# Score steps of the first three tiles in single PSUM banks, four in flight, in place of two bank pairs

## The chip, the cores and the metric

The kernel runs on one core of a Trainium2 chip. The metric is device time in microseconds (us), the median of several runs. All times of a trace count from the start of its span. The engines are named as in the profile: PE (TensorE matmuls), PEld (its weight loads), DVE (VectorE), ACT (ScalarE), POOL (GpSimd), SP (SyncE, which here issues the DMAs).

## What is computed

Block-causal attention, then a mixture of four experts, then one dense layer with a softmax gate and a layer norm:

```python
scores = scale * q @ k.T, masked by blocks of 64 (i >= j)     # 4 batches, 8 heads, 576 positions, width 64
attn = exp(scores - max) / (sum + 1e-9);  x = attn @ v        # x: 2304 x 512
out = sum over 4 experts e of p[:, e] * (relu(x @ w1[e]) @ w2[e])      # 512 -> 1024 -> 512
h = out @ w_in;  solu = h * softmax(h);  y = layernorm(solu) * g @ w_out
```

## The kernel before

The 2304 rows are 18 tiles of 128. `TILES[t] = (b, i)`: tiles 0 and 1 take the first 64 positions of two batches each (i = 0), tile 2 is (0, 1), tile 3 is (0, 2), tile 4 is (0, 3), tile 5 is (0, 4), and so on. A tile is computed in attention steps: tiles 0 and 1 have two steps of four heads (steps 0 to 3), tile 2 has four steps of two heads (4 to 7), tile 3 has steps 8 to 11, tile 4 has 12 to 15, and tile 5 has eight steps of one head (16 to 23).

A step has three parts. `step_a` multiplies q with k on PE into the PSUM tile `sps` (a high and a low part of q, L902 and L903 in tiles 0 and 1, L920 and L923 later, and a masking product); then DVE takes the maximum (L932 or L935, written into free words of the same PSUM tile) and turns it into the exponent's bias `nm` (L939). `step_b` lets ACT do the exponential head by head (L979); while `t < DIRECT`, with `DIRECT = 3`, the result goes back in place into PSUM. ACT copies it to half precision in `hl` (L992), DVE subtracts for the rest (L993), and SP transposes `hl` by DMA into `pT`. `step_c` multiplies `pT` with v on PE (`pv`, L1021). After the last step of a tile, `finish` normalises it on DVE (L1057 to L1063), splits it (`xh`, L1074 on ACT, L1075 on DVE), and SP transposes it into `xT`.

The scores go through a pool of two PSUM tiles of two banks each; a step gives its tile back when its last subtraction L993 has run. `hl` has two buffers (`hlp=2`), q has four (`qp=4`).

As soon as tiles are ready, the experts' matmuls fill PE between the steps: `emit_h` (`hps`, L375: 96 matmuls for one tile, 128 columns each) and `emit_o` (`ops`, L397: 24 matmuls of 512 columns for one tile). Their weights are loaded into `stage`, squared on ACT for a scale (L132), summed (L217), multiplied by ones on PE (`tp`, L219), turned into `ws` on DVE (L221, L136, L140, L143), and split in four chunks: the high part `wt` on POOL (L231) for the first expert and on ACT (L235) for later ones, the low part on DVE (L238). POOL also converts q and k (`qhi`, `qlo`, `ks`, L798 and L800) and v (L881; its low part on DVE is L882).

The program's order up to tile 2 is a hand-written string of tokens; then a planner mixes attention steps and expert units by their costs. The framework's scheduler then sets each engine's instruction order from a simulated timeline and the priorities of that program order. Each engine runs its own list strictly in that order.

Of the kernel before, what the change touches and what calls it, by code (L numbers as in the profile page):

```python
# [7 lines left out]
F32 = mybir.dt.float32  # L8
# [9 lines left out]
PSUM = bass.MemoryType.PSUM  # L18
# [14 lines left out]
DIRECT = 3  # L33
# [30 lines left out]
def tile_kernel(  # L64
# [19 lines left out]
    class InOrder:  # L84


        def __init__(self, eng):
            self.eng, self.last = eng, None
# [655 lines left out]
    class Attention:  # L744


        def __init__(self, bufs):
            self.es = es = ExitStack()
            self.nraw = {k: bufs[k] for k in ("qr", "kr")}
            for n, k in bufs.items():  # L750
                setattr(self, n, es.enter_context(tc.tile_pool(name=n, bufs=k)))
            self.pss = es.enter_context(tc.tile_pool(name="pss", bufs=2, space=PSUM))
            self.psv = es.enter_context(tc.tile_pool(name="psv", bufs=4 - NPH, space=PSUM))
            self.kS, self.qS, self.vS, self.vSc, self.raws = {}, {}, {}, {}, {}
            self.sPS, self.hl_, self.nm_, self.pT_, self.sums, self.xps = {}, {}, {}, {}, {}, {}
            self.steps = []
            for t in range(NTILE):
                i = TILES[t][1]
                if i == 0:
                    self.steps += [(t, c, tuple(range(4 * c, 4 * c + 4)), True) for c in range(2)]  # L760
                elif i < 4:
                    self.steps += [(t, p, (2 * p, 2 * p + 1), True) for p in range(4)]
                else:
                    for p in range(4):
                        self.steps += [(t, p, (2 * p,), False), (t, p, (2 * p + 1,), True)]
            self.first = {}
            for n, st in enumerate(self.steps):
                self.first.setdefault(st[0], n)
            self.NS = len(self.steps)
            self.fin = []  # L770
            self.n = self.na = self.nb = self.nc = self.nhl = 0
            self.todo = []
            self.plan()

            self.todo.sort(key=lambda x: x[0])
            self.loads = {k: [l for _, (x, l), _ in self.todo if x == k] for k in self.nraw}
            self.nl = {k: 0 for k in self.nraw}
            self.done = {k: 0 for k in self.nraw}
# [107 lines left out]
        def step_a(self, n):  # L886
            t, p, heads, _ = self.steps[n]
            b, i = TILES[t]
            ps = self.pss.tile([128, 2, 512], F32, tag="s", name="sps")
            self.sPS[n] = ps  # L890
            nm = sp.tile([128, 4], F32, tag="nm", name="nm")
            self.nm_[n] = nm
# [35 lines left out]

            def rest():
                if i == 0:  # L930
                    mx = ps[:, 1, 0:4]
                    vec.tensor_reduce(out=mx, in_=v4, axis=AX.X, op=ALU.max, negate=True)  # L932
                elif i < 4:
                    mx = ps[:, :, 511]
                    vec.tensor_reduce(out=mx, in_=ps[:, :, 0:L], axis=AX.X, op=ALU.max, negate=True)  # L935
                else:
                    mx = nm[:, 0:1]
                    vec.tensor_reduce(out=mx, in_=ps[:, :, 0:288], axis=AX.XY, op=ALU.max, negate=True)
                vec.tensor_scalar(  # L939
                    out=nm[:, 0:nh], in0=mx, scalar1=SCALE, scalar2=PBITS * LN2, op0=ALU.mult, op1=ALU.add  # L940
                )
# [317 lines left out]
    def norm():  # L1259
# [11 lines left out]
        w=p0[:5], x=p1[:5], W=p0[5:] + q0, X=p1[5:] + q1, P=[norm],  # L1271
# [108 lines left out]
    while at1.more:  # L1380
        t, u, cost = moe[-1] if moe else (-1, None, 0)
        ok = t is None or t in ready and len(bg) <= n1
        if not ok or tdv <= tpe + 2.0:
            flush()
            at1.step()
            a, c = at1.cost()
# [233 lines left out]
```

## Time and profile before

| | |
|---|---|
| median of 3 runs | 1090.99 us (1089.95 to 1091.23) |
| the profiled execution | 1090.29 us, its span 1088.5 us |
| PE busy | 1041.5 us, 96% of the span |
| DVE, ACT, POOL busy | 776.3, 511.1, 208.1 us |

The profiled execution is 0.70 us below the median of the runs, and 1.79 us of it lie outside the span. A row of the timeline gives the start, the duration, the engine and line, what is written and read, how many instructions are merged into the row, and in brackets how long the engine stood idle before it and what ended that.

### The profile page before, as it was taken

The numbers are of one execution on the slowest core, as the hardware profiler recorded it, in microseconds if no ns is written. First come the engines' busy times: TensorE is split into PE (matmuls) and PEld (weight loads), VectorE is DVE, ScalarE is ACT, GpSimd is POOL, SyncE is SP. The second block draws the span as 40 slices with busy tenths as digits, with TensorE's granted clock in tenths as the row PEclk, the third lists the DMA queues.
The fourth block names the chain that finished last, engine by engine and source line by source line (L and its number), as shares of the span: only waits on it lengthen the run. The fifth ranks groups of instructions, "written<-read, shape, count | busy, mean of one in ns | idle before, by whom it ended". The sixth has DMA issues, their size and how long they took to land.

```text
span 1088.5 us, 20680 instructions
## 1 busy us (share of the span) xinstructions
PE 1041.5 (96%) x8088; PEld 657.0 (60%) x8088; DVE 776.3 (71%) x1758; ACT 511.1 (47%) x1108; POOL 208.1 (19%) x280
## 2 busy tenths in 40 slices
PE   4679899999999999999899999999999999999998
PEld 4556666656655655655476777776766674444444
DVE  6879677748767765545786557665879558999883
ACT  5757578546755454532353334231446353323322
POOL 4967733534237311000000000000000000000000
PEclk9989999999999999999999999999999999999999
DMA  9978997566677865235331211330346312435233
GB/s 295 277 175 167 241 201 189 143 173 172 158 178 174 186 112 129 56 90 157 122 97 51 77 47 55 117 136 30 98 145 167 77 24 36 88 88 106 60 87 87
DMA packets 225745, 137.96 MB, mean 127 GB/s; under 512 B 184560, under 2 KB 193008, under 8 KB 225648
## 3 DMA queue, kind: packets, MB, share of 16 engines
q1 hardware_dynamic: 225648, 136.65, 50.3%
q8 instruction: 63, 1.03, 0.4%
q14 instruction: 34, 0.28, 0.1%
HBM read 79.47 MB, written 12.06 MB: 84 GB/s over the span
## 4 chain that ended last, share of the span: by engine, by line
PE 84%; DMA 6%; DVE 4%; POOL 3%; ACT 1%; issue 1%; SPq 0%; DVEq 0%; ACTq 0%; POOLq 0%
PE ops L397 31%; PE hps L629 14%; PE hps L375 14%; PE o L1536 9%; PE h L1470 9%; PE pv L1021 3%; DMA pT<-hl 3%; PE sps L920 2%; PE sps L923 2%; DMA xT<-xh 1%; POOL ks L800 1%; DMA raw<-in_w_dram 1%; DMA x2T<-xh 1%; DMA near<-in_kT_dram 1%; DMA vraw<-in_vC_dram 1%
## 5 line engine op out<-in xcount | busy, mean ns | idle before, releaser
L397 PE MATMUL ops<-wt,hch 128*128 128x512 f16 x1728 | 393.1, 379 | 2.4 <-DVE wt L238 1.4
L397 PEld LDWEIGHTS <-hch 128*128 128x128 f16 x1728 | 166.1, 98 | 187.4 <-issue 6.7
L375 PE MATMUL hps<-xT,wt 128*128 128x384 f16 (+1 forms) x1536 | 216.1, 290 | 6.3 <-DVE hch L386 3.9
L375 PEld LDWEIGHTS <-wt 128*128 128x128 f16 x1536 | 126.5, 100 | 64.4 <-issue 6.1
L979 ACT ACTIVATE p<-sps,nm 128x320 f32<-128x320 f32 (+3 forms) x120 | 70.1, 587 | 85.1 <-DVE nm L939 75.4
L993 DVE TENSOR_TENSOR hl<-p,hl 128x320 f16<-128x320 f32 (+3 forms) x120 | 75.6, 650 | 37.3 <-ACT hl L992 37.2
L629 PEld LDWEIGHTS <-S 128*128 128x128 f16 x1152 | 96.0, 98 | 3.0 <-issue 0.9
L1536 PE MATMUL o<-wt,lt 128*128 128x512 f16 (+1 forms) x456 | 95.6, 368 | 0.0
L1470 PE MATMUL h<-wt,x2T 128*128 128x512 f16 x432 | 95.5, 379 | 0.0
L238 DVE SCALAR_TENSOR_TENSOR wt<-stage,ws,wt 128x1024 f16<-128x1024 f32 (+1 forms) x64 | 82.9, 1304 | 7.4 <-ACT wt L235 4.3
L422 DVE SCALAR_TENSOR_TENSOR acc<-ops,coef,acc 128x512 f32<-128x512 f32 x54 | 40.4, 748 | 66.4 <-PE ops L397 66.3
L920 PE MATMUL sps<-ks,qhi 128*128 128x288 f32 (+3 forms) x160 | 69.1, 433 | 10.7 <-DVE hl L993 7.5
L629 PE MATMUL hps<-T,S 128*128 128x192 f16 x864 | 76.3, 246 | 0.0
L629 PEld LDWEIGHTS <-wt 128*128 128x128 f16 x864 | 72.8, 98 | 5.8
L642 ACT ACTIVATE stu<-hps 128x384 f32<-128x384 f32 x72 | 34.6, 482 | 86.5 <-PE hps L629 86.3
L1536 PEld LDWEIGHTS <-lt 128*128 128x128 f16 x456 | 44.6, 98 | 48.9
L1470 PEld LDWEIGHTS <-x2T 128*128 128x128 f16 x432 | 42.3, 98 | 51.0
L386 DVE SCALAR_TENSOR_TENSOR hch<-hps,hch 128x384 f16<-128x384 f32 (+1 forms) x98 | 52.8, 540 | 21.9 <-ACT hch L385 21.8
L647 ACT ACTIVATE hch<-stc 128x384 f16<-128x384 f32 x72 | 37.4, 521 | 63.5 <-DVE stc L655 63.2
L385 ACT ACTIVATE hch<-hps 128x384 f16<-128x384 f32 (+1 forms) x98 | 46.9, 481 | 39.5 <-PE hps L375 39.4
L1021 PE MATMUL pv<-v,pT 128*128 128x64 f16 x1392 | 56.6, 196 | 8.9 <-DMA pT<-hl 8.8
L1021 PEld LDWEIGHTS <-pT 128*128 128x128 f16 x1392 | 51.6, 100 | 20.5 <-DMA pT<-hl 10.8
(163 smaller groups left out, 1534.6 us busy)
## 6 DMA issues: line engine op xcount, KB each, us to landing
stage<-in_w_dram SPq DMA_DIRECT2D x50, 512.0 KB, 5.9
raw<-in_qT_dram SPq DMA_DIRECT2D x34, 256.0 KB, 3.1
vraw<-in_vC_dram SPq DMA_DIRECT2D x30, 256.0 KB, 3.2
raw<-in_kT_dram SPq DMA_DIRECT2D x24, 288.0 KB, 3.5
raw<-in_w_dram SPq DMA_DIRECT2D x24, 256.0 KB, 4.1
raw<-in_w_in_dram SPq DMA_DIRECT2D x8, 512.0 KB, 4.7
raw<-in_w_out_dram SPq DMA_DIRECT2D x8, 512.0 KB, 4.2
stage<-wf SPq DMA_DIRECT2D x8, 512.0 KB, 6.6
```

What stands on the lines that cost most here:

```text
L238: stage["last"] = vec.scalar_tensor_tensor(out=lo, in0=r, scalar=stage[key, "s"], in1=hi, op0=ALU.mult, op1=ALU.subtract)
L375: pe.matmul(ps[:, j * n:j * n + n], w[:, a, kk, f * 128:(f + 1) * 128], x[:, b * KD + kk, c0:c0 + n], start=(m == 0), stop=(m == 3 * KD - 1),)
L385: marks["A"] = nc.scalar.activation(out=h[:, 0, :n], in_=ps[:, :n], func=AF.Relu)
L386: marks["D"] = nc.vector.scalar_tensor_tensor(out=h[:, 1, :n], in0=ps[:, :n], scalar=0.0, in1=h[:, 0, :n], op0=ALU.max, op1=ALU.subtract)
L397: pe.matmul(ps, hch[f][:, a, o0:o0 + 128], w[:, b, f, :], start=(m == 0), stop=(m == 3 * KF - 1))
L629: i = pe.matmul(ps[x][:, jj * HT:jj * HT + HT], lhs(a, kk, jj), rhs(b, kk), start=start, stop=(m == 5), skip_group_check=not first or jj > 0,)
L920: pe.matmul(o, q, rhs, start=True, stop=False)
L979: act.activation(out=src if direct else dst, in_=src, func=AF.Exp, bias=nm[:, j + x:j + x + 1], scale=SCALE, accum_out=sums[:, h:h + 1],)
L993: anc["D"] = vec.tensor_tensor(out=lo, in0=pf, in1=hi, op=ALU.subtract)
L1021: pe.matmul(o, tt[:, a * nch + c, :], v[:, bb, hs], start=(m == 0), stop=(m == total - 1))
L1470: pe.matmul(ps[:, half], x[:, a * KD + kk, c:c + 128], w[:, b, kk, half * 512:half * 512 + 512], start=(m == 0), stop=(m == 3 * KD - 1),)
L1536: pe.matmul(ps, tt[:, x * KF + f], w[:, y, f, c], start=(m == 0), stop=(m == 3 * KF - 1))
```

## The change

In tiles 0 to 2 a step now takes one PSUM bank from a new pool of four. In tiles 0 and 1 it needed only one bank anyway (four heads of 128 columns), and its maximum goes to `nm` in SBUF. In tile 2 the two heads of 192 columns lie side by side in one bank, and the two maxima in that bank's last two words. When the first step of tile 3 is built, the pool of single banks is closed, and the former pool of two bank pairs is opened over the same four banks.

```diff
-            self.pss = es.enter_context(tc.tile_pool(name="pss", bufs=2, space=PSUM))
             self.psv = es.enter_context(tc.tile_pool(name="psv", bufs=4 - NPH, space=PSUM))
+            self.one = ExitStack()
+            self.ps1 = self.one.enter_context(tc.tile_pool(name="ps1", bufs=4, space=PSUM))
+            self.pss = None
...
-            ps = self.pss.tile([128, 2, 512], F32, tag="s", name="sps")
+            spare = None
+            if t < DIRECT:
+                bank = self.ps1.tile([128, 512], F32, tag="s", name="sps")
+                w = 1 if i == 0 else 2
+                ps = bank[:, 0:512 if i == 0 else 128 + 256 * i].rearrange("p (a c) -> p a c", a=w)
+                if i:
+                    spare = bank[:, 510:512]
+            else:
+                if self.pss is None:
+                    self.one.close()
+                    self.pss = self.es.enter_context(tc.tile_pool(name="pss", bufs=2, space=PSUM))
+                ps = self.pss.tile([128, 2, 512], F32, tag="s", name="sps")
...
                 if i == 0:
-                    mx = ps[:, 1, 0:4]
+                    mx = nm
...
-                    mx = ps[:, :, 511]
+                    mx = ps[:, :, 511] if spare is None else spare
```

The scheduler answers with another order of instructions on all engines for the first part of the program (lines below `step_a` are 13 higher in the change, and those above it 2 higher). Three places matter here.

On DVE, where the first expert's scale `ws_207` is made: `wt1_311` is the sum of the squares, `v_277` the low part of tile 1's values, `hl_337` the remainder of step 2. Before:

```order
L217 TENSOR_REDUCE wt1_311<-wt4_206 128x1
L882 SCALAR_TENSOR_TENSOR v_277<-qv_137,vs_257,v_277 128x512
L221 COPY wt2_315<-tp_313 128x1
L136 TENSOR_SCALAR iw_93<-wt2_315 128x1
L140 TENSOR_SCALAR iw_93<-iw_93 128x1
L143 RECIPROCAL ws_207<-iw_93 128x1
L573 RECIPROCAL ss_7190<-iw_93 128x1
L573 RECIPROCAL ss_7391<-iw_93 128x1
L993 TENSOR_TENSOR hl_337<-sps_320,hl_337 128x512
```

The same place in the change (`sps_549` belongs to step 5):

```order
L948 TENSOR_REDUCE sps_549<-sps_549 128x2
L952 TENSOR_SCALAR nm_494<-sps_493 128x2
L143 RECIPROCAL vs_257<-vinv_258 128x1
L217 TENSOR_REDUCE wt1_311<-wt4_206 128x1
L952 TENSOR_SCALAR nm_550<-sps_549 128x2
L221 COPY wt2_315<-tp_313 128x1
L884 SCALAR_TENSOR_TENSOR v_277<-qv_137,vs_257,v_277 128x512
L136 TENSOR_SCALAR iw_93<-wt2_315 128x1
L1006 TENSOR_TENSOR hl_337<-sps_320,hl_337 128x512
L140 TENSOR_SCALAR iw_93<-iw_93 128x1
L143 RECIPROCAL ws_207<-iw_93 128x1
```

The maxima of steps 4 and 5 now come before the scale, and the two long instructions `v_277` and `hl_337` stand inside its chain.

On DVE again, at the first step of tile 3 (step 8: `sps_777`, `nm_778` before, `sps_781`, `nm_782` in the change); `wt_560` are chunks of w2 of the first expert. Before:

```order
L935 TENSOR_REDUCE sps_777<-sps_777 128x2
L386 SCALAR_TENSOR_TENSOR hch_780<-hps_779,hch_780 128x256
L238 SCALAR_TENSOR_TENSOR wt_560<-stage_268,ws_270,wt_560 128x1024
L939 TENSOR_SCALAR nm_778<-sps_777 128x2
L935 TENSOR_REDUCE sps_876<-sps_876 128x2
```

In the change:

```order
L1006 TENSOR_TENSOR hl_703<-sps_651,hl_703 128x192
L238 SCALAR_TENSOR_TENSOR wt_560<-stage_268,ws_270,wt_560 128x1024
L948 TENSOR_REDUCE sps_781<-sps_781 128x2
L238 SCALAR_TENSOR_TENSOR wt_560<-stage_268,ws_270,wt_560 128x1024
L952 TENSOR_SCALAR nm_782<-sps_781 128x2
L948 TENSOR_REDUCE sps_880<-sps_880 128x2
```

Before, the bias of step 8 stood behind the third of the four chunks; now it stands behind the fourth, and behind the last remainder of tile 2 (`hl_703`, step 7).

On PE, at the last step of tile 3 (step 11: `sps_982` before, `sps_986` in the change); `xT_477` holds tiles 0 to 2, `hps_1034` is tile 1, `pv_956` and `pv_960` are tile 3's products with v. Before:

```order
L375 LDWEIGHTS wt_415
L375 MATMUL hps_1034<-xT_477,wt_415 128x128
L920 MATMUL sps_982<-ks_443,qhi_763 128x320
L1021 LDWEIGHTS pT_825
L1021 MATMUL pv_956<-v_648,pT_825 128x64
```

In the change (`ops_1286` is tile 1's output product):

```order
L1034 LDWEIGHTS pT_829
L1034 MATMUL pv_960<-v_459,pT_829 128x64
L933 MATMUL sps_986<-ks_440,qhi_763 128x320
L936 MATMUL sps_986<-ks_440,qlo_764 128x320
L938 LDWEIGHTS mr_88
L938 MATMUL sps_986<-mc_89,mr_88 128x64
L933 MATMUL sps_986<-ks_443,qhi_763 128x320
L936 MATMUL sps_986<-ks_443,qlo_764 128x320
L938 LDWEIGHTS mr_88
L938 MATMUL sps_986<-mc_89,mr_88 128x64
L397 LDWEIGHTS hch_1126
L397 MATMUL ops_1286<-wt_560,hch_1126 128x512
```

Before, step 11 stood in the middle of tile 1's `hps` and was itself split by the product `pv` of step 8. In the change it stands behind all 96 `hps` of tile 1, behind the first 9 of its 24 `ops`, and behind that `pv`.

## Rows read from the trace of the kernel before

**Rows 1.** The page, part 1: busy time, share of the span, instructions of each engine.

```profile
PE 1041.5 (96%) x8088; PEld 657.0 (60%) x8088; DVE 776.3 (71%) x1758; ACT 511.1 (47%) x1108; POOL 208.1 (19%) x280
```

**Rows 2.** Stretches: bounds, length; PE, PEld, DVE, ACT, POOL busy; clock, DMA share, GB/s.

```profile
0.00:45.00 45.00, 20.96 (x130) 19.10 (x131) 33.25 (x90) 30.62 (x89) 28.65 (x38) 1.00 1.01 293
...
52.50:72.50 20.00, 13.16 (x124) 8.54 (x122) 16.29 (x29) 11.54 (x33) 18.61 (x18) 0.96 0.62 131
72.50:77.50 5.00, 5.00 (x48) 4.44 (x48) 2.73 (x5) 3.31 (x10) 2.01 (x4) 0.50 1.17 299
77.50:90.00 12.50, 12.50 (x142) 8.46 (x142) 9.23 (x19) 9.11 (x26) 2.53 (x4) 0.99 0.98 207
90.00:120.00 30.00, 27.72 (x400) 22.72 (x399) 28.96 (x62) 22.56 (x47) 25.95 (x33) 1.00 0.82 205
120.00:152.00 32.00, 26.36 (x356) 20.20 (x355) 21.47 (x54) 15.64 (x54) 21.02 (x33) 1.00 1.11 221
152.00:1088.50 936.50, 928.34 (x6805) 566.09 (x6802) 657.01 (x1483) 414.47 (x842) 101.89 (x146) 1.00 0.44 110
```

**Rows 3.** Waits of PE from 20 to 152 us: total, times, longest.

```profile
PE pv L1021 <- DMA pT<-hl: 8.8, 6, 2.3
PE sps L920 <- DVE hl L993: 7.5, 4, 2.2
```

**Rows 4.** Timeline of PE: step 4, tile 0's hps, step 11's end, two prices.

```profile
27.85 0.50 PE L920 MATMUL sps<-ks,qhi 128*128 128x192 f32 x1 [1.92 <-DVE hl L993]
...
45.05 2.82 PE L375 MATMUL hps<-xT,wt 128*128 128x128 f16 x25 [0.43 <-DMA xT<-xh]
...
73.78 0.28 PE L925 MATMUL sps<-mc,mr 128*128 128x64 bf16 x1
...
78.64 2.62 PE L375 MATMUL hps<-xT,wt 128*128 128x128 f16 x44
...
85.44 3.19 PE L397 MATMUL ops<-wt,hch 128*128 128x512 f16 x14
```

**Rows 5.** Timeline of ACT: step 4's copy, second head of step 6, step 8's exponential.

```profile
34.97 0.33 ACT L992 ACTIVATE hl<-sps 128x192 f16<-128x192 f32 x1 [1.20 <-DMA pT<-hl]
...
50.81 0.40 ACT L979 ACTIVATE sps<-sps,nm 128x192 f32<-128x192 f32 x1 [2.09 <-DVE hl L993]
...
61.88 0.53 ACT L979 ACTIVATE p<-sps,nm 128x320 f32<-128x320 f32 x1 [4.78 <-DVE nm L939]
```

**Rows 6.** Timeline of DVE around the scale, tile 2's first-head remainder, step 8's bias.

```profile
25.55 0.75 DVE L882 SCALAR_TENSOR_TENSOR v<-qv,vs,v 128x512 f16<-128x512 f32 x1 [0.26 <-POOL v L881]
...
26.79 0.17 DVE L143 RECIPROCAL ws<-iw 128x1 f32<-128x1 f32 x1
...
27.01 0.69 DVE L993 TENSOR_TENSOR hl<-sps,hl 128x512 f16<-128x512 f32 x1
...
50.44 0.34 DVE L993 TENSOR_TENSOR hl<-sps,hl 128x192 f16<-128x192 f32 x1
...
63.89 1.52 DVE L238 SCALAR_TENSOR_TENSOR wt<-stage,ws,wt 128x1024 f16<-128x1024 f32 x1 [1.30 <-POOL wt L231]
```

**Rows 7.** Timeline of POOL: first chunk, one wait, fourth chunk of w2, one conversion.

```profile
27.05 2.21 POOL L231 TENSOR_SCALAR wt<-stage,ws 128x1024 f16<-128x1024 f32 x2 [1.53 <-DVE ws L143]
...
32.64 1.10 POOL L798 TENSOR_SCALAR qhi<-raw 128x512 fp32r<-128x512 f32 x1 [0.46 <-PE sps L920]
...
62.74 1.12 POOL L231 TENSOR_SCALAR wt<-stage,ws 128x1024 f16<-128x1024 f32 x1
63.82 0.51 POOL L798 TENSOR_SCALAR ks<-raw 128x384 fp32r<-128x384 f32 x1
```

**Rows 8.** Waits of POOL from 71 to 92 us, and of DVE from 74 to 90 us.

```profile
POOL qhi L798 <- PE sps L920: 13.1, 3, 6.6
...
DVE sps L935 <- PE sps L925: 3.8, 4, 1.6
```

**Rows 9.** Groups of DVE instructions from 90 to 120 us: busy, mean ns, idle before.

```profile
L238 DVE SCALAR_TENSOR_TENSOR wt<-stage,ws,wt 128x1024 f16<-128x1024 f32 x4 | 5.2, 1295 | 0.0
```

## Prediction

> **What bounds the kernel now.** I read the page's busy times first, then a table by stretch, then the waits of PE, then the timelines of the engines that PE waits for. PE is busy for 1041.5 of 1088.5 us [rows 1], and the table says where the rest is: after 152 us it idles 8.2 us in 936.5, so from there on the kernel is its matmuls, and nothing that happens earlier matters except through the time at which that stretch is reached [rows 2]. Idle time lies ahead of it: 24.0 us up to 45 us, 6.8 us from 52.5 to 72.5, 2.3 us from 90 to 120, 5.6 us from 120 to 152 [rows 2]. A change of the first three tiles can gain only there. One more loss does not show as idle: from 72.5 to 77.5 us PE is busy throughout, but at the granted clock 0.50, the lower level of 1.2 GHz [rows 2].
>
> Who is waited for? From 20 us on the second largest wait of PE is 7.5 us, in 4 pieces, of scores for the subtraction L993, which gives a PSUM pair back [rows 3]. That is the wait which four single banks take away. Whether it is worth 7.5 us is another matter. Three of the four pieces lie ahead of 45 us, where the experts' first matmuls begin, and what these wait for is the transpose of tile 0 [rows 4], which steps 4 to 7 don't feed. Scores that come early there only wait elsewhere: step 4's copy into half precision waited 1.20 us for a transpose to give back one of two `hl` buffers [rows 5], and that limit stays. From 52.5 to 72.5 us POOL is busy for 18.6 of 20 us [rows 2]: it makes the chunks of w2 and the k of tile 3, and these pace the stage.
>
> **Earlier scores, tiles 0 to 2.** Steps 2 to 7 no longer wait for L993 (step 4 did so for 1.92 us, until 27.85 [rows 4]). They move up as far as their q and k allow. I cost the gain from this itself at nothing: what hides it is tile 0's chain of normalising, splitting and transposing, which ends at 45.05 in any case [rows 4]. Without that cover it would be the 7.5 us [rows 3]. The new place of the maxima and the narrower layout keep the shapes of the operations, so they cost nothing either.
>
> **The scale of the first expert comes later.** The moved maxima push work into the chain of `ws`: `v_277` (0.75 us) and `hl_337` (0.69 us) now stand inside it [rows 6]. Before, `v_277` stood beside the PE product `tp`, ahead of its copy; now it stands behind that copy with nothing beside it. The bounds are thus 0.69 and 1.44 us; I take 1.2, near the upper one. POOL begins the chunks when `ws` is there, at 27.05 with an idle of 1.53 us just for it [rows 7], and is then nearly saturated, so its chain moves by 1.2. Ahead of w2's fourth chunk POOL now has two more conversions of k, 0.51 us each [rows 7], and it loses the wait of 0.46 us for scores of step 5 [rows 7]. Together 1.2 + 1.0 - 0.5 = 1.7 us: the fourth chunk ends at 63.9 + 1.7 = 65.6 [rows 7]. The bounds are 0 (if ACT, no longer held up in the squares of the weights, gives the time back) and what follows if all of tile 3 goes as late as its first step. That one's bias now stands behind the fourth chunk's low part (1.52 us [rows 6]): 65.6 + 1.5 + 0.2 = 67.3 for its exponential, which ran at 61.88 [rows 5]. So 5.4 is the other bound. I take 1.7, because the later steps of tile 3 waited for POOL's k anyway, of which the change makes two heads sooner.
>
> **PE's gaps are filled.** Counted in both orders, PE now has 192 `hps` and 33 `ops` ahead of step 11, where it had 124 and 24: 68 `hps` and 9 `ops` more, nearly all of tile 1. At 2.62/44 and 3.19/14 us each [rows 4] that is 4.05 + 2.05 = 6.1 us of work. Step 11 ended at 74.06 [rows 4], and from 52.5 to 72.5 us PE was idle for 6.8 us [rows 2], so there is room for it. The two bounds: 0, if PE waits for chunks and transposes just as long with the new order, and the room itself, 6.8.
>
> The sum: 6.1 - 1.7 = 4.4 us less at step 11. Does it last until 152 us? From 90 to 120 DVE is busy for 28.96 of 30 us [rows 2], and 5.2 us of that are the low parts of the next expert's w1 [rows 9]. In the new order these four stand between steps 12 and 13, in the stretch from 72.5 to 90, where DVE had 5.5 us idle [rows 2], 3.8 of it waiting for scores, while POOL waited 13.1 us for them [rows 8]. The attention steps can thus make up there what they lost. I let the 4.4 stand, without a gain for the freed DVE (bound: the 2.3 us that PE idled from 90 to 120 [rows 2]). Against its own execution: 1090.29 - 4.4 = 1085.9; that execution is 0.70 below the median of the runs, so the median should come to 1086.6.
>
> **A rule that speaks against it.** With both heads in one bank, the exponential of the second and the subtraction of the first can't overlap, if the engines must take turns. The trace says that they take turns already: the second head of step 6 was exponentiated at 50.81, after 2.09 us of waiting for L993 [rows 5], and that L993, of the first head, had begun at 50.44 [rows 6], although the two heads lay in different banks. So the one bank costs nothing new. The Trainium skill, "PSUM — Partial Sum Buffer", section "PSUM bank collisions raise a hardware error", says that two engines may not access one bank in the same quadrant of partitions at a time, so that software has to guard whole banks. By that rule alone, tile 2's four steps would each get longer by one copy and one subtraction, an estimate of 4 x (0.33 + 0.34) = 2.7 us from the rows just named, and the sum would be 1.7 us instead of 4.4. The trace pays it before the change too, so I keep 4.4.
>
> **Rivals.** (a) The forecast, 1086.6, on its own 1084.5 to 1088.5: chance 0.36.
>
> (b) The half clock goes too. It fell after the stretch in which PE stood idle for a third of the time [rows 2]; with the gaps filled it may stay up. The 5 us at half then shrink to 2.5: 1084.1. Against it: PE still waits between chunks. Chance 0.17.
>
> (c) Given back. PE's longest waits are for the transposes of `hl`, 8.8 us in 6 pieces [rows 3], most of them after 100 us, set by DMA and by the order in SP's queue. Work done early is missing there as filler, and PE waits longer for the same tiles. Then the end doesn't move: 1091, give or take 2. For it: the transposes' order is untouched in kind. Against it: the next weights' load and split move ahead of that stretch. Chance 0.23.
>
> (d) Slower. Tile 3 takes the full delay of its first step, 5.4 us, and keeps it, because its bias is queued behind a chunk that POOL brings later, and PE then meets the `pv` of step 8 ahead of step 11 without its transpose. The tiles behind come later by as much, and the filler of 6.1 us has been spent by then. Between 1.7 and 5.4 us late at 152 us, in the middle 3.5: 1094.5. It decides from the point where step 11 ends more than 6.1 us later than 74.06, that is after 80.2. Chance 0.24.
>
> **How the numbers follow.** A measurement of this kernel can tell 0.2%, 2.2 us, from no change. (a) and (b) are faster, but for a piece of (a), about 0.02, that ends within the bound: 0.51. (c) gives 0.22 of no change with 0.01 to the slower side, (a)'s piece and the near end of (d), 0.02, join it: 0.26. Slower: 0.23. Cases of both signs hold most of the chance, so the range reaches from (b) with 2 us to spare to (d)'s middle: 1082 to 1094.5.
>
> **What would show it.** Right: step 4 starts some 6 us ahead of 27.85; tile 0's `hps` still begin near 45; the first chunk on POOL begins near 28.3; from 52.5 to 72.5 PE idles under 2 us, with `hps` of tile 1 in it; step 11 ends near 76. Wrong in size: the first chunk no later than 27 (then about 1.7 us better), or `hps` of tile 0 well off 45, which would mean that the early scores do feed the front. Wrong altogether: waits of `pv` for transposes between 100 and 152 us that grow by the gain, or step 8's exponential at 67 and everything behind it 5 us late.

## The result, and the profile after

The changed kernel takes 1098.08 us in the median (1095.16 to 1099.73), the kernel before, run beside it on the same chip, 1090.47 (1089.12 to 1091.23): a ratio of 1.0075, with the interval 1.0054 to 1.0097. That is 7.6 us slower, where 4.4 us faster were forecast, and it lies above the range. The profiled execution is the fastest of its four, 1095.16, with a span of 1093.4 us; against the span of before that is 4.9 us. What the two traces can explain are these 4.9; the remaining 2.7 are the scatter of the new kernel's executions.

By the busy times of the page, DVE, ACT and POOL do what they did, within 3 us [rows 1]. PE is busy 3.9 us longer for the same number of matmuls, and idle 48.0 us in place of 47.0: most of the 4.9 us is matmuls that ran slower.

```profile
PE 1045.4 (96%) x8088; PEld 658.4 (60%) x8088; DVE 777.2 (71%) x1758; ACT 512.2 (47%) x1108; POOL 205.3 (19%) x280
```

The table by stretch of the changed kernel, with the columns of [rows 2]; the line from 150 to 165 is an extra one inside two others:

```profile
0.00:45.00 45.00, 22.34 (x138) 19.84 (x139) 34.22 (x98) 30.37 (x91) 27.79 (x37) 1.00 0.94 284
52.50:72.50 20.00, 16.68 (x170) 11.23 (x168) 14.04 (x22) 8.13 (x24) 18.35 (x18) 0.91 0.72 161
72.50:77.50 5.00, 3.42 (x38) 2.36 (x38) 3.29 (x12) 5.00 (x16) 0.00 (x0) 1.00 0.93 225
77.50:90.00 12.50, 10.38 (x113) 7.26 (x110) 10.32 (x23) 11.33 (x25) 4.05 (x8) 0.90 0.77 152
90.00:120.00 30.00, 26.83 (x363) 21.50 (x362) 25.46 (x56) 20.14 (x47) 17.80 (x27) 0.99 0.98 198
120.00:152.00 32.00, 26.36 (x357) 19.84 (x355) 25.07 (x52) 16.05 (x52) 26.55 (x36) 1.00 0.99 220
150.00:165.00 15.00, 13.45 (x171) 10.89 (x172) 10.63 (x28) 12.57 (x38) 2.18 (x4) 0.89 0.93 180
152.00:1093.40 941.40, 932.86 (x6840) 569.92 (x6840) 658.92 (x1491) 417.50 (x851) 103.39 (x150) 1.00 0.44 110
```

The same table of the kernel before, for the one stretch that no group ahead has:

```profile
150.00:165.00 15.00, 14.81 (x190) 10.94 (x190) 8.98 (x22) 14.20 (x38) 2.68 (x5) 1.00 0.92 187
```

The reader is to see three things. First, from 52.5 to 72.5 us PE's idle time fell from 6.84 to 3.32 us, where under 2 were forecast: gaps were filled, but a part of the busy time is slow work, at a granted clock of 0.91 in place of 0.96. Second, the half clock of 72.5 to 77.5 is not gone. It has moved, to three places (three stretches of the changed kernel, with the columns of [rows 2]):

```profile
57.00:60.00 3.00, 3.00 (x9) 1.10 (x8) 2.71 (x5) 1.88 (x6) 2.92 (x3) 0.50 0.24 39
87.50:90.50 3.00, 3.00 (x25) 2.56 (x25) 1.67 (x2) 2.69 (x7) 2.06 (x4) 0.50 0.11 25
152.50:155.50 3.00, 3.00 (x21) 2.41 (x21) 1.86 (x5) 2.78 (x9) 1.08 (x3) 0.50 0.86 212
```

By (1 - clock) x length, summed over the lines of the tables, half clock cost an estimated 5.0 us after and 3.4 before. Over all runs the difference is larger: the mean clock of the change's four runs is 0.995 and three times 0.994, that of the runs of the kernel before 0.996 to 0.997, so that by the same estimate 2 to 3 of the 7.6 us are half clock. Third, the idle time comes back at once: 1.6 us from 72.5 to 77.5 and 2.1 from 77.5 to 90, where there was none, and 3.2 from 90 to 120 in place of 2.3. And from 150 to 165 us, where the kernel before was at full clock and nearly free of gaps, PE now idles 1.55 us at a granted clock of 0.89.

The timeline of PE after, by the rows that answer to [rows 4] and by the places where time is lost:

```profile
18.82 0.51 PE L933 MATMUL sps<-ks,qhi 128*128 128x192 f32 x1
...
61.71 0.39 PE L933 MATMUL sps<-ks,qhi 128*128 128x320 f32 x1
...
78.68 0.20 PE L938 MATMUL sps<-mc,mr 128*128 128x64 bf16 x1
...
86.44 0.70 PE L1034 MATMUL pv<-v,pT 128*128 128x64 f16 x18 [2.12 <-DMA pT<-hl]
...
97.32 0.48 PE L933 MATMUL sps<-ks,qhi 128*128 128x448 f32 x1 [1.09 <-ACT p L992]
...
150.66 0.52 PE L1034 MATMUL pv<-v,pT 128*128 128x64 f16 x12 [1.81 <-DMA pT<-hl]
152.07 0.49 PE L375 MATMUL hps<-xT,wt 128*128 128x128 f16 x4 [0.89 <-DMA xT<-xh]
...
174.50 0.38 PE L219 MATMUL tp<-wt,ones 128*128 128x1 f32 x2 [1.91 <-DVE wt L217]
```

Step 4 begins at 18.82 in place of 27.85, step 11 ends at 78.88 in place of 74.06 (with 6.1 us more work ahead of it), and the first expert's `hps` for tile 5 begin at 152.07. Of the waits from 20 to 152 us, the one for the subtraction is down from 7.5 us to 1.2, and that for the transposes of `hl`, 8.8 in [rows 3], stands nearly where it stood:

```profile
PE pv L1034 <- DMA pT<-hl: 8.5, 6, 2.1
...
PE sps L933 <- DVE hl L1006: 1.2, 2, 0.9
```

For [rows 5 to 7], the timelines of ACT, DVE and POOL have these: the first chunk of w2, step 7's last subtraction, the fourth chunk and its low part, step 8's bias and exponential.

```profile
28.07 2.21 POOL L231 TENSOR_SCALAR wt<-stage,ws 128x1024 f16<-128x1024 f32 x2 [1.80 <-DVE ws L143]
...
60.10 0.34 DVE L1006 TENSOR_TENSOR hl<-sps,hl 128x192 f16<-128x192 f32 x1
...
64.72 1.11 POOL L231 TENSOR_SCALAR wt<-stage,ws 128x1024 f16<-128x1024 f32 x1
65.87 1.28 DVE L238 SCALAR_TENSOR_TENSOR wt<-stage,ws,wt 128x1024 f16<-128x1024 f32 x1 [0.76 <-POOL wt L231]
67.07 0.15 DVE L952 TENSOR_SCALAR nm<-sps 128x2 f32<-128x2 f32 x1
69.02 0.51 ACT L992 ACTIVATE p<-sps,nm 128x320 f32<-128x320 f32 x1
```

The waits of POOL from 71 to 92 us and of DVE from 74 to 90 us answer to [rows 8], the group of DVE from 90 to 120 us to [rows 9]: two low parts of w1 are still there, of four.

```profile
POOL qhi L800 <- PE sps L933: 14.7, 2, 7.6
...
DVE sps L948 <- PE sps L938: 1.3, 1, 1.3
```

```profile
L238 DVE SCALAR_TENSOR_TENSOR wt<-stage,ws,wt 128x1024 f16<-128x1024 f32 x2 | 3.1, 1546 | 0.0
```

**Lost time.** Since the change reorders PE's work, the same step starts at another time merely because other work stands ahead of it. To compare, I take the start of a step's first score and subtract the work that stands ahead of it in PE's order, at the prices of full clock: 0.0553 us for an `hps` (groups of 44 and of 22 give (2.62 - 1.40)/22 = 0.0555), 0.2136 for an `ops` (groups of 14 and of 5 give (3.19 - 1.24)/9 = 0.217), 0.0292 for a `pv`, and scores in proportion to their columns. What is left is time in which PE waited or ran slower; differences between rows are good to some 0.3 us. In us (the rows below the second are the experiments of the next section):

| at the start of step | 8 | 12 | 15 | 23 | 28 | 32 | 36 |
|---|---|---|---|---|---|---|---|
| before | 42.8 | 50.8 | 51.0 | 53.5 | 58.3 | 60.2 | 60.1 |
| after | 45.5 | 49.2 | 54.1 | 58.1 | 59.8 | 64.9 | 67.0 |
| e5, two groups of banks | 41.6 | 49.1 | 50.4 | 51.9 | 59.2 | 67.8 | 67.7 |
| e6, banks of before, other order | 42.9 | 47.8 | 51.3 | 56.7 | 61.3 | 66.1 | 69.3 |
| e7, one idle pair taken | 43.5 | 52.5 | 52.3 | 59.9 | 62.7 | 68.3 | 68.3 |
| e15, three banks | 45.2 | 53.6 | 53.3 | 58.3 | 61.5 | 69.2 | 69.2 |
| e13, other order behind 141 us | 43.2 | 50.7 | 50.5 | 52.8 | 57.4 | 59.5 | 60.7 |
| e17, after with a short tile 5 | 46.0 | 50.4 | 55.1 | 58.7 | 61.4 | 63.1 | 63.7 |
| e18, before with a short tile 5 | - | 48.6 | 48.9 | 52.1 | 57.2 | 57.3 | 57.7 |

The changed kernel is 1.6 us ahead at step 12 (82.35 us), 3.1 behind at step 15 (97.32), 1.5 behind at step 28 (138.13), 4.7 at step 32 (158.17) and 6.9 at step 36 (180.45); about 2 of these come back by the end. Between steps 28 and 32 lies the first expert's tile 5. There the change loses 5.1 us and the other slow kernels of the table (e5, e6, e7, e15) 4.8 to 8.6, while the kernel before, e13, e17 and e18 lose 0.1 to 2.1.

### The profile page after: what moved, and what is told of

Its sections match the earlier page's. It is cut to its first block, busy times and chain, and to the rows that moved or that the text cites. A ratio compares the mean times of both kernels' runs of the same rounds, so it can differ in the third digit from the quotient of the medians.

```text
span 1093.4 us, 20671 instructions
## 1 busy us (share of the span) xinstructions
PE 1045.4 (96%) x8088; PEld 658.4 (60%) x8088; DVE 777.2 (71%) x1758; ACT 512.2 (47%) x1108; POOL 205.3 (19%) x280
## 4 chain that ended last, share of the span: by engine, by line
PE 81%; DMA 7%; DVE 5%; POOL 4%; issue 1%; ACT 1%; SPq 1%; DVEq 0%; POOLq 0%; ACTq 0%
PE ops L397 31%; PE hps L629 14%; PE hps L375 13%; PE o L1549 9%; PE h L1483 9%; DMA pT<-hl 3%; PE pv L1034 3%; PE sps L933 2%; PE sps L936 1%; DMA vraw<-in_vC_dram 1%; POOL v L883 1%; DVE hl L1006 1%; DMA xT<-xh 1%; POOL ks L802 1%; POOL wt L231 1%
## 5 line engine op out<-in xcount | busy, mean ns | idle before, releaser
L1549 PEld LDWEIGHTS <-lt 128*128 128x128 f16 x456 | 44.6, 98 | 48.9
L1034 PEld LDWEIGHTS <-pT 128*128 128x128 f16 x1392 | 50.8, 100 | 21.1 <-DMA pT<-hl 11.5
```

The lines of the kernel that those rows point to most:

```text
L1034: pe.matmul(o, tt[:, a * nch + c, :], v[:, bb, hs], start=(m == 0), stop=(m == total - 1))
L1549: pe.matmul(ps, tt[:, x * KF + f], w[:, y, f, c], start=(m == 0), stop=(m == 3 * KF - 1))
```

## The experiments

Ratios are against the kernel before, run beside each on the same chip, with 95% intervals. The expectations name theories as they stood when each was written; some of these fell.

**Is it the layout?** e1 keeps the two pairs and puts both heads into one bank of a pair. The order of instructions is that of before on every engine.

```diff
 ps = self.pss.tile([128, 2, 512], F32, tag="s", name="sps")
...
+if t < DIRECT:
+    bank = ps[:, 0]
...
+    ps = bank[:, 0:512 if i == 0 else 128 + 256 * i].rearrange("p (a c) -> p a c", a=w)
```

> The layout alone: the steps of the first three tiles put both heads into one bank of a pair, and the second bank of the pair stays unused, so that no more steps are under way than before; every engine's order of work is that of before. Theory S (the switch: the changed kernel loses because step 8's first pair can only be formed when the last subtraction of tile 2 has given its bank back): no change, 1089.5 to 1091.5 us. Rival L (the layout: two heads in one bank make tile 2's steps longer): slower by the 2.7 us that the prediction worked out or more, 1093 or above. Rival F (filler: the early scores let the experts' matmuls of tiles 0 and 1 run too early, and they are missing later): no change, as S.

Measured: 1090.18 us, 1.0007 (0.9994 to 1.0020). Two heads in one bank, and the maxima elsewhere, cost nothing. What is slower must come with the four banks: with their switch to pairs, or with the order that they bring. The Trainium skill, "PSUM — Partial Sum Buffer", section "PSUM bank collisions raise a hardware error", has software guard PSUM by bank and quadrant of partitions, in the simple version by whole banks. Here that guard costs nothing, since ACT and DVE took turns over a step's two heads before [rows 5, 6].

**Other ways to four banks.** e2 lets two steps in a row share a pair; e3 lets steps 4 and 7, and 5 and 6, share one, so that a pair comes free sooner; e4 takes single banks for the first two tiles only.

```diff
 # e2
+    if n % 2 == 0:
+        self.pair = self.pss.tile([128, 2, 512], F32, tag="s", name="sps")
+    bank = self.pair[:, n % 2]
...
 # e3
+    if n in (0, 2, 4, 5):
+        self.pair[n] = self.pss.tile([128, 2, 512], F32, tag="s", name="sps")
+    bank = self.pair[(0, 0, 2, 2, 4, 5, 5, 4)[n]][:, n in (1, 3, 6, 7)]
...
 # e4
-            if t < DIRECT:
+            if t < 2:
```

> Four steps under way as in the changed kernel, but without the switch: the pairs stay throughout, and two neighbouring steps of the first three tiles share one, a bank each. Step 8 then waits for steps 4 and 5 alone. Theory S: step 8's scores return from 61.7 us to 56 or earlier, and the time falls to 1087 to 1091. Rival L: two heads lie in one bank as in the changed kernel, so as slow as that one, 1095 to 1099. Rival F: the scores come early as in the changed kernel, so 1095 to 1099 too.

> As the kernel with shared pairs, but the four steps of tile 2 share them crosswise: steps 4 and 7 one pair, steps 5 and 6 the other. One of tile 3's first two steps then waits for the last subtraction of tile 2 again (step 9 here, and step 8 for that of step 6). Theory S: the loss comes back in part, 1092 to 1098, and at least 2 us above the kernel with shared pairs. Rivals L and F: the same as the kernel with shared pairs within 1.5 us.

> The changed kernel with single banks for tiles 0 and 1 only; tile 2 takes pairs as before. The switch then lies ahead of step 4, where the last subtraction of tile 1 ends near 31 us, and step 8 waits for step 6 as before. Theory S: 1089 to 1092. Rival L: tile 2 has no shared bank, so no change either, 1089 to 1092. Rival F: the scores of tile 1 alone come earlier, a part of the loss stays, 1093 to 1096.

Measured: e2 1106.79 us, 1.0147 (1.0118 to 1.0176); e3 1104.35, 1.0131 (1.0106 to 1.0155); e4 1102.47, 1.0112 (1.0087 to 1.0137). All three moved more than they were meant to. Tile 0's `hps`, at 45.05 before and 44.22 after, begin at 57.94, 55.66 and 51.54: the front became late, which it is not in the change. The timeline of PE in e2:

```profile
54.70 0.21 PE L1031 MATMUL pv<-v,pT 128*128 128x64 f16 x1 [7.01 <-POOL v L881]
...
57.94 4.53 PE L375 MATMUL hps<-xT,wt 128*128 128x128 f16 x48
```

They say that the front is worth its time when it is late, and nothing on the change itself. e4 shows the one wait that the change adds: its switch lies ahead of step 4, which starts at 32.06 after PE waited 4.20 us for the last subtraction of tile 1, because the pairs open only when all four single banks are back. The timeline of PE in e4:

```profile
32.06 0.50 PE L933 MATMUL sps<-ks,qhi 128*128 128x192 f32 x1 [4.20 <-DVE hl L1006]
```

**Is it the late switch to pairs?** In the change step 8's scores are held up in the same way: step 7's subtraction runs at 60.10 and step 8 starts at 61.71, where it started at 55.30 before. e5 makes two groups of two single banks, each of which becomes its own pair.

```diff
-            self.ps1 = self.one.enter_context(tc.tile_pool(name="ps1", bufs=4, space=PSUM))
...
+            self.ps1 = [x.enter_context(tc.tile_pool(name=f"ps1{k}", bufs=2, ...)) for k, x in enumerate(self.one)]
...
+                if self.pss[n % 2] is None:
+                    self.one[n % 2].close()
```

> The changed kernel without its switch as a whole: two groups of two single banks, each of which becomes one pair for itself. Everything up to step 7 is issued in the changed kernel's order; step 8 waits for steps 4 and 5 alone, step 9 for step 7. Theory S (the loss is step 8's wait for the last subtraction of tile 2): step 8's scores run near 56 us instead of 61.7, and the time is 1088 to 1092. Rival O (the order as such: after any shift the scheduler deals the work of tiles 3 to 5 out anew, and the order of the kernel before is a good one that any other misses by some us): 1094 to 1104, wherever step 8 runs.

Measured: 1098.06 us, 1.0065 (1.0049 to 1.0081). Step 8 starts at 53.04, earlier than before the change, and the kernel is as slow as with the late switch. Up to step 23 it is ahead of the kernel before by 0.6 to 1.7 us (table); then PE runs out of work:

```profile
53.04 0.39 PE L933 MATMUL sps<-ks,qhi 128*128 128x320 f32 x1
...
128.06 4.38 PE L375 MATMUL hps<-xT,wt 128*128 128x128 f16 x41 [4.46 <-DMA xT<-xh]
```

It waits 4.46 us for one transpose, and the 41 `hps` behind it take 4.38 us, where 44 took 2.62 [rows 4]. In e5 the later steps of tile 3 are still late (step 9's exponential at 69.25 in place of 66.17), but the tile as a whole is not: its `xf` begins at 87.65, before at 89.19, after at 91.59. So a late tile 3 is not needed for the loss.

**Is it the order as such?** e6 is the kernel before with its banks, and puts the second halves of the steps of tiles 2 and 3 first. e7 is the kernel before and takes one pair for an idle product, and a copy out of it, ahead of step 8.

```diff
 # e6
...
+            with tc.high_priority(offset=PRI if self.steps[n][0] in (2, 3) else 0):
+                self.step_b_(n)
 # e7
+            if n == 8:
+                idle = self.pss.tile([128, 2, 512], F32, tag="s", name="idle")
+                pe.matmul(idle[:, 0, 0:1], ones, ones[:, 0:1], start=True, stop=True)
...
```

> The kernel before, with its own pairs, and only the priority of the softmax of tiles 2 and 3 raised in the scheduler. Every engine's order is that of before up to step 10, near 68 us; from there on the scheduler deals it out anew, without any change of banks. Theory S: no loss, 1088 to 1092, since step 8 stands where it stood. Rival O: 1094 to 1104, as for the other orders.

> The kernel before with one idle pair taken ahead of step 8 (one matmul of one column and one copy of one column more), so that step 8 takes the pair of step 7, and step 9 that of step 6. The two come back within 0.3 us of each other, so step 8 is hardly later, but the order behind it is dealt out anew. Theory S: 1088 to 1092.5. Rival O: 1094 to 1104.

Measured: e6 1098.66 us, 1.0074 (1.0059 to 1.0089); e7 1097.80, 1.0069 (1.0051 to 1.0086). In e6 PE's order is that of before up to about 67 us, and no bank is laid out anew; its price is that of the change. So an order alone can cost as much. It loses its time in waits for transposes at 118 and 138 us:

```profile
118.00 1.78 PE L1030 MATMUL pv<-v,pT 128*128 128x64 f16 x30 [3.03 <-DMA pT<-hl]
...
138.07 1.78 PE L1030 MATMUL pv<-v,pT 128*128 128x64 f16 x30 [3.29 <-DMA pT<-hl]
```

**Does work done early pay at all?** If PE has a given amount of filler and must wait for tile 5 in any case, then less work ahead of that point would not let it come sooner. e8 leaves out two of three products of the first expert for tiles 1 and 2, in the kernel before (14.9 us of PE's work); e9 does so for tile 5 alone; e10 and e11 are the same two with the change.

```diff
+            ab = ((0, 0),) if k == 1 and t0 in (1, 2) else ((0, 0), (0, 1), (1, 0))
...
-                for a, b in ((0, 0), (0, 1), (1, 0)):
+                for a, b in ab:
```

> The kernel before, without two of the three products of the first expert for tiles 1 and 2: 128 hps and 32 ops fewer, 7.6 + 7.3 = 14.9 us of PE's work, all of it ahead of 150 us; the result lacks those parts. Theory G (gate: up to some 150 us PE works off the first expert's tiles 0 to 4 and then waits for the xT of tile 5, which the attention steps set; what PE does ahead of that earlier or not at all only lengthens its waits): the hps of tile 5 still begin at 149 to 157 us, and the time is 1088 to 1097. Rival P (PE's work counts wherever it lies): 1075 to 1078.

> The kernel before, without two of the three products of the first expert for tile 5: 64 hps and 16 ops fewer, 3.8 + 3.6 = 7.4 us of PE's work, behind the point where its xT lands; the result lacks those parts, and the order up to that point is that of before. Theory G: the full 7.4 us come off, 1081 to 1084. Rival P: the same. It is the measure for the leaving out ahead of the gate.

> The changed kernel, with the same left out for tiles 1 and 2 (14.9 us of PE's work ahead of 150 us). Theory G: the hps of tile 5 begin at 150 to 158 us, and the time is 1090 to 1099. Rival P: 1083 to 1085.

> The changed kernel, with the same left out for tile 5 (7.4 us of PE's work behind the gate). Theory G: 1089 to 1092, so that the changed kernel stays 6 to 9 us behind the kernel before with the same left out. Rival P: the same.

Measured: e8 1096.18 us, 1.0058 (1.0040 to 1.0076); e9 1105.90, 1.0147 (1.0121 to 1.0173); e10 1105.44, 1.0148 (1.0133 to 1.0163); e11 1103.50, 1.0123 (1.0106 to 1.0140). With 14.9 us of work less ahead of it, PE begins tile 5's `hps` at

```profile
149.64 2.17 PE L376 MATMUL hps<-xT,wt 128*128 128x128 f16 x36 [0.72 <-DMA xT<-xh]
```

in place of 150.19. So this point is set by the attention's chain, and hardly by how much of the filler is done. What I had not expected is e9: the program has less work and takes 16 us more. It meets waits between 154 and 173 us (1.43, 3.26, 2.57, 2.39), and the granted clock falls with them; the kernel before had 1.00 in both stretches. e10 and e11 lie above every range that was stated for them, too.

```profile
150.00:165.00 15.00, 10.30 (x103) 6.81 (x104) 9.81 (x21) 13.45 (x37) 2.54 (x5) 0.86 0.82 179
165.00:180.00 15.00, 10.05 (x81) 6.89 (x81) 10.95 (x27) 13.56 (x30) 5.00 (x8) 0.57 0.89 176
```

As a measure of what filler is worth, these four failed, since leaving work out brought new waits and half clock. They suggest that PE's work near tile 5 is the cover under which the attention's waits lie.

**Where in the order?** e12 and e13 let `pv` follow its scores by two steps, not three, from tile 4 on, in the change and in the kernel before; PE's order then differs behind some 141 us. e14 moves only the second halves of tile 2's steps. e15 is the change with three single banks.

```diff
 # e12, e13
-            return 3 if 4 <= t < LATE else 2 if 2 <= t < FREE else LAG
+            return 2 if 4 <= t < LATE else 2 if 2 <= t < FREE else LAG
 # e14
+            with tc.high_priority(offset=PRI if self.steps[n][0] == 2 else 0):
 # e15
-            self.ps1 = self.one.enter_context(tc.tile_pool(name="ps1", bufs=4, space=PSUM))
+            self.ps1 = self.one.enter_context(tc.tile_pool(name="ps1", bufs=3, space=PSUM))
```

> The changed kernel with the lag of pv behind the scores cut from 3 steps to 2 for the tiles 4 to 11. PE's order is that of the changed kernel up to the last products of the first expert for tile 4, near 148 us; behind it some 2 to 10 us more of the experts' matmuls stand ahead of the steps from 170 to 190 us. Theory T (tail: a good part of the loss arises behind 148 us, where too few experts' matmuls stand between the steps, PE waits and the clock drops): 1093 to 1096, at least 2 us below the changed kernel. Rival E (early: all of it is lost by 148 us): no change, 1097 to 1099.

> The kernel before with the same cut of the lag: PE's order is that of before up to 147 us and is dealt out anew behind it. Theory T: its filler behind 148 us stays as rich as before (within 3 us at each step), so no change, 1088 to 1091.5. Rival O (any new order costs some 7 us): 1095 or above.

> The kernel before with the priority of tile 2's softmax alone raised: only four hps of PE, a piece of POOL's k and q of tile 3 and a few issues of SP change places near 64 to 70 us; all the rest of the order is that of before. Theory T: no change, 1088 to 1091.5. Rival O in its strictest form (any swap costs): 1094 or above.

> The changed kernel with three single banks in place of four. Its experts' matmuls ahead of the steps from 170 to 190 us are those of the kernel before (115.7, 122.9 and 131.6 us of work ahead of three steps of tile 8, against 117.6, 122.9 and 131.6 before and 113.5, 116.8 and 122.1 with four banks), but ahead of tile 5 it has 49.7 us of work, like the changed kernel (49.6; before 39.9). Theory T: 1090 to 1094. Rival E (what counts is how early the filler is used up ahead of tile 5): 1097 to 1100.

Measured: e12 1100.57 us, 1.0098 (1.0075 to 1.0121); e13 1091.47, 1.0017 (1.0005 to 1.0030); e14 1089.26, 0.9995 (0.9979 to 1.0011); e15 1098.94, 1.0076 (1.0052 to 1.0101). The theory behind e12, that the shorter lag would mend the change, falls. Another order behind 141 us costs the kernel before 0.17%, and the small exchange of e14 nothing, so that not every other order costs. Three banks cost what four do, which is what rival E gave, and not the theory. In e12 tile 5 stands where it stood in the change, at 152.09, and the wait for the chain of the next scale is there again:

```profile
152.09 0.40 PE L375 MATMUL hps<-xT,wt 128*128 128x128 f16 x4 [0.87 <-DMA xT<-xh]
...
175.17 0.38 PE L219 MATMUL tp<-wt,ones 128*128 128x1 f32 x2 [2.54 <-DVE wt L217]
```

**Is it tile 5's transpose?** The chain behind the attention of tile 5 runs from `xf` (135.71 before, 137.09 after) over the scale to the low part of `xh` (145.43, 147.20), then SP issues the transpose. e16 is the kernel before with the squares of that chain done five times. e17 is the change without tile 5's scale, with that of tile 4 in its place. e18 does the same to the kernel before.

```diff
 # e16
-                squares(x, T, xh[:, 1].bitcast(BF16))
+                for _ in range(5 if t == 5 else 1):
+                    squares(x, T, xh[:, 1].bitcast(BF16))
 # e17, e18
+                if t == 5:
+                    return
...
+                s_, inv_ = self.four if t == 5 else (s, inv)
```

> The kernel before, with the squares of tile 5's finish taken five times instead of once (four more of 0.8 us on ACT), so that its xT lands later; the order is that of before up to about 140 us. Theory G (the first wait that the experts cannot cover is that for the xT of tile 5, near 150 us; what makes it later makes the kernel slower): the xT lands 2.5 to 3.5 us later, near 153, and the time is 1092 to 1097. Rival N (PE comes to that place about when the xT lands by chance, and it has other work to do): 1089 to 1091.5.

> The changed kernel, with the finish of tile 5 shortened: it takes tile 4's scale in place of its own, which leaves out one pass of squares on ACT and three small operations on DVE, each of which waits in its queue. Everything up to about 124 us is in the changed kernel's order. Theory G: the xT of tile 5 lands at 146 to 149 us instead of 152, and the time falls by 3 us or more, to 1091 to 1095. Rival N: 1097 to 1099.

> The kernel before with the same shortened finish of tile 5. PE waited there for 1.87 us alone. Theory G: at most those 1.9 us, so 1087.5 to 1090; the gain is smaller than that of the changed kernel. Rival N: no change, 1089 to 1090.5.

Measured: e16 1091.63 us, 1.0010 (0.9992 to 1.0028); e17 1092.42, 1.0029 (1.0008 to 1.0049); e18 1089.18, 0.9989 (0.9974 to 1.0005). SP's queue issued tile 5's transpose, in the kernel before, the change, e16 and e17, one fence each:

```profile
146.46 1.23 SPq L94 DMA_TRANSPOSE xT<-xh  x1
```

```profile
148.11 1.89 SPq L94 DMA_TRANSPOSE xT<-xh  x1
```

```profile
147.44 1.23 SPq L94 DMA_TRANSPOSE xT<-xh  x1
```

```profile
143.21 1.23 SPq L94 DMA_TRANSPOSE xT<-xh  x1
```

In e17 PE no longer waits for this transpose, keeps the full clock from 150 to 165 us, and waits 0.73 us for the next scale in place of 1.91:

```profile
150.00:165.00 15.00, 14.23 (x183) 10.64 (x181) 11.29 (x27) 12.96 (x38) 3.95 (x8) 1.00 1.02 214
```

```profile
169.42 0.35 PE L219 MATMUL tp<-wt,ones 128*128 128x1 f32 x2 [0.73 <-DVE wt L217]
```

The same edit moves the change by -0.46% (1.0075 to 1.0029, 5.0 us) and the kernel before by -0.11% (1.2 us, within what can be told from nothing). So 4 to 5 us of the change's 7.6 go with this edit; by the two intervals, each of these differences is uncertain by 2 to 3 us. e16 was to show the reverse, and did not: the dose came out at 1.0 us of delay, less than the 1.65 of the change, and its price, if there is one, is within the interval. From 126 us on the orders of e17 and of the change differ, too. From step 33 to step 36 PE has as much work ahead in e17 as in the kernel before, about 4 us more than the change has ahead of step 36. So e17 does not single out the transpose.

## Why the prediction was wrong

**What was right.** The early scores are there, 9 us ahead (6 forecast), and worth nothing in themselves: tile 0's `hps` begin within 1 us of where they began. The first chunk of w2 is at 28.07 (28.3 forecast, 27.05 before); the low part of the fourth begins 2.0 us later (1.7 forecast). The layout costs nothing (e1).

**Mis-sized: tile 3.** Step 8's exponential is 7.1 us late, beyond the bound of 5.4. Its bias, at 67.07, is where the working had it, behind the low part of the fourth chunk. The scores start 6.4 us later, since the pairs open only when step 7's subtraction is through, but they are done by 62.7 and are not what the bias waits for. What the bound left out is a place in ACT's queue: squares of v, whose load comes late, stand ahead of the exponential. The timeline of ACT after:

```profile
68.39 0.63 ACT L132 ACTIVATE vraw<-vraw 128x512 f32<-128x512 f32 x1 [2.87 <-DMA vraw<-in_vC_dram]
```

This is not what decided: in e5 that exponential runs at 60.32, earlier than before, and the ratio stays at 1.0065.

**Mis-sized: the filling.** It is there, with idle time halved from 52.5 to 72.5 us. The half clock of 72.5 to 77.5, which rival (b) saw going, came back at three other places and cost more than before. At step 12 the lost time is down by 1.6 us, not by 4.4.

**The step that failed: "Does it last until 152 us? ... I let the 4.4 stand."** By step 15 the gain has turned into a loss of 3.1 us (waits of 2.12 us for a transpose at 86.44 and 1.09 for ACT at 97.32, and a granted clock of 0.90 from 77.5 to 90). Up to about 150 us PE has nothing to fill its waits with but the first expert's tiles 0 to 4, and then it waits for tile 5, whose time the attention's chain sets: e8 speaks for that, with the point at 149.64 in spite of 14.9 us less work. Work done early is then not time gained; it is filler that is missing later, and idle time only moves. So far this is rival (c), though the sign stated for it is faint: the waits of `pv` for transposes between 100 and 152 us come to 6.4 us in place of 5.9. And (c) had the end where it was; the rest of the price lies where I did not look. The attention arrives 1.4 us late at tile 5 (`xf`) and its transpose is issued 1.65 us late. PE waits 1.81 and 0.89 us there, where the kernel before waited 1.87 and kept the full clock. It then runs from 150 to 165 at a granted clock of 0.89, and meets a wait of 1.91 us for the next scale at 174.50. The lost time grows from 1.5 us more than before, at step 28, to 6.9 at step 36. In e17, with tile 5's chain shortened and another order behind it, most of that goes (1.0029).

**Rival (d)**, slower by a late tile 3, gave 1094.5 and ends on the right side, but by another mechanism than the measured one: its condition, step 11 ending after 80.2, isn't met (78.88), and e5 is as slow with tile 3 finished earlier than before.

**What is shown, and what stays open.** Shown: that the layout is free (e1); that the loss needs neither the late switch nor a late tile 3 (e5); that another order with the banks of before costs as much (e6 1.0074; e7 1.0069, with one product and one copy more), so that an order alone is enough for a loss of this size.

Argued, not shown: that the change's own loss is that of its order between 68 and 148 us and not of the four banks, since no run has four banks in the order of before; and that 4 to 5 of the 7.6 us hang on tile 5's chain, since e17 changes the order as well. Nor can the late attention be the whole of it: in e12 the `xf` of tile 5 is only 0.5 us late (136.17) and the kernel is no faster than the change, and in e17 it is 3.6 us late (139.34).

One rival was left untested. The second expert's products are PE's next stock of work; they begin at 166.34 us before, 174.74 after and 169.63 in e17. They need a scale whose four squares (L132) run on ACT. The last of the four, before, after and in e17, one fence each:

```profile
164.64 1.06 ACT L132 ACTIVATE junk<-stage 128x1024 bf16<-128x1024 f32 x1
```

```profile
171.53 1.05 ACT L132 ACTIVATE junk<-stage 128x1024 bf16<-128x1024 f32 x1
```

```profile
167.93 1.06 ACT L132 ACTIVATE junk<-stage 128x1024 bf16<-128x1024 f32 x1
```

The first of the four begins at 164.93 in the change and at 164.39 in e17. In e17 and before, the four stand one behind the other; in the change the attention's exponentials and copies stand between them. Of the kernels that compute the whole result, all the slow ones (the change, e2 to e7, e12, e15) begin these products at 174 us or later, and all the others (e1, e13, e14, e16 to e18) before 170. Whether these late squares are a cause of the loss or only a mark of it is open; the change with its four squares held together would tell.

Nor is it shown which single exchange makes the attention or the squares late, and why the order of before fits best among nearly all that were tried. The last 3 us, which e17 keeps (lost time 63.1 against 60.2 at step 32), were not traced to one move either.

## What to carry to other kernels

Where one engine fills its waits from a fixed stock of work and then meets a point that a chain of short steps sets, work brought forward can be worth nothing, as here, until that chain is faster: look for the first wait that the filler can't cover, and price a change by what it does to that. A change of a pool deals out the scheduler's whole order anew, so test the layout with the order held, and the order with the layout held, before explaining anything by the edited lines. Idle time or half clock that vanishes in one stretch has to be followed to the next few, with the work ahead of each step subtracted.

## What the runs showed of the hardware

Waits on PE were in several places followed by stretches at the lower clock of 1.2 GHz, so that they cost more than their length. 30 `pv` took 1.78 us behind waits of 3.03 and of 3.29 us (e6, with a granted clock of 0.50 from 118.0 to 119.8 and from 138.05 to 139.85), and 41 `hps` 4.38 us behind one of 4.46 (e5, 0.53 from 128.0 to 132.45). At full clock as many took 1.05 us in the kernel before and 2.45 in the change:

```profile
124.08 1.05 PE L1021 MATMUL pv<-v,pT 128*128 128x64 f16 x30 [0.84 <-DMA pT<-hl]
```

```profile
93.78 2.45 PE L375 MATMUL hps<-xT,wt 128*128 128x128 f16 x41
```

Not every such wait was followed by it: in the kernel before, 24 `pv` behind a wait of 2.28 us, at 105.54, took 0.87 us at a granted clock of 1.00, while in the change half clock followed one of 2.12 (86.44). In e9, which leaves out work of PE and takes 16 us more, the granted clock was 0.86 and 0.57 in two stretches of 15 us where the kernel before had 1.00, an estimated 8.6 us by (1 - clock) x length.

Up to about 50 us the clock column doesn't tell the rate. It reads 1.00 in both kernels, but the first 25 `hps` before took 2.82 us [rows 4] and the first 40 after, at 44.22, took 4.43 us: 0.11 us each, twice the price of full clock.
